# Paired 64-row matmuls on halves of the array become one full 128-row matmul per block of hidden units

## The chip, the cores and the metric

The kernel runs on one core of one Trainium2 chip. The metric is the time of one execution on the device in microseconds (us); the kernel before was run three times.

## The reference

Three stages follow each other: a recurrent attention (mLSTM), a mixture of eight experts with a greedy assignment of tokens, and a dense block.

```python
# attention: 4 batch rows, 8 heads, 768 steps, 40 dims; y = o * (C q) / max(|n q|, 1)
x = y.transpose(0, 2, 1, 3).reshape(3072, 320)
# experts: each takes the 384 tokens that the greedy order of all logits gives it
logits = x @ w_gate
for e in range(8):
    h = np.maximum(x[mask_e] @ w1[e], 0.0)        # 320 -> 1024
    out[mask_e] = h @ w2[e]                       # 1024 -> 320
# dense block on every token
h = out @ w_in                                    # 320 -> 2048
g = np.where(h > 0.0, h, np.exp(np.minimum(h, 0.0)) - 1.0)
return g @ w_out                                  # 2048 -> 320
```

## The kernel before, in words

The attention (class `Attention`) fills the first 224 us. After it come eight rounds (class `Mlp`), one for each expert: a round gathers the 384 tokens of its expert, runs the expert (8 blocks of 128 hidden units) and then the dense block on the same tokens (16 blocks). Class `Router` finds the tokens of the later rounds at the same time; its steps are short products on TensorE (PE, L691, L748, L769, L804 to L806, L831) between chains of small operations on VectorE (DVE).

Every float32 operand is kept as two parts of half the bits, a high one and a low one, and a product of two operands takes three passes: high by high, low by high, high by low. The inner dimension of the first product of both the expert and the dense block is 320, that is two chunks of 128 rows and a last one of 64. `Mlp.up` (L1110) writes one block of 128 hidden units by 384 tokens into a bank of PSUM. For the two chunks of 128 it needs six matmuls (L1118 to L1127). For the last 64 rows the weights `ws` (`w1s` of the expert, `wis` of the dense block) hold both parts above each other: in an even block rows 0 to 63 are the high part and rows 64 to 127 the low one, in an odd block the other way round. The inputs `xh[:, 2]` and `xl[:, 2]` hold the 64 rows twice, above each other. So L1130 does high by high and low by high in one matmul of 128 rows. What is left is high by low, 64 rows. An even block `f` does it for itself on one half of the array (L1136) and for block `f + 1` on the other half (L1137); for that it opens the bank of block `f + 1` ahead of that block's other matmuls:

```python
PE.matmul(p, ws[:64, c], xl[:64, 2], start=False, stop=True)
PE.matmul(self.open_[f + 1][0], ws[64:, c.stop:c.stop + 128], xl[64:, 2], start=new, stop=False)
```

There are (8 + 16) * 8 = 192 blocks, so 96 such pairs. Block by block, `P1` hands the bank to a ReLU (L1157 and L1164) and `P2` to an elu (`elu`: L1189, L1190 on ScalarE, ACT; L1193 on DVE, which is the last reader of the bank; then L996 and L1002, which split the result into `gh` and `gl`). `C1` (L1234 to L1249) and `C2` (L1278 to L1282) take the split blocks three blocks later for the second product. Four banks (`ph`) take turns among the blocks of `up` and the transposes of the next round's tokens (`prep_x`, L1071).

The order of all instructions is settled when the program is built. `Plan` keeps an estimate of each engine's time: `plan.pe(n, cols)` adds n matmuls of `cols` columns to PE's, and the router's steps, the next round's tokens and weights, and the operations that DVE, ACT or GpSimd (POOL) can each do, are put where that estimate says. Each engine then works through its own list in order and waits on semaphores.

Of the kernel before, what the change touches and what calls it, by code (L numbers as in the profile page):

```python
# [18 lines left out]
NR, CAP, TK = 8, 384, 384  # L19
# [16 lines left out]
class Plan:  # L36
    """An estimate of when the engines come to what is emitted (ns), so that nothing is emitted long before its
    operands are there, and what two engines can do goes to the one that is free first."""
# [14 lines left out]
    def on(self, e, ns, after=0):  # L53
        """the time after ns on engine e"""
        self.at[e] = max(self.at[e], self.t, after) + ns
        return self.at[e] + HOP
# [30 lines left out]
class Ring:  # L87
    """The tiles of a tag that take turns: the next one's place is free once its last reader is emitted"""
# [7 lines left out]
    def free(self, k):  # L96
        """whether the next k places are free by now"""
        q = self.q[-self.n:]
        return all(x[0] and x[0] <= self.plan.t for x in q[:max(0, len(q) - self.n + k)])
# [10 lines left out]
def spread(ap, parts):  # L110
    """a run of DRAM for every partition"""
    return bass.AP(tensor=ap.tensor, offset=ap.offset, ap=[[0, parts]] + [list(x) for x in ap.ap])


class Attention:
    """mLSTM by chunks of 128 steps; a unit is a chunk of a batch row with its eight heads"""

    def __init__(self, nc, tc, consts, dram, qko, vk, ig, fg, wg, pad, xd, L, ident):
# [17 lines left out]
        def spin(n):  # L136
            """products of no use that keep the tensor engine's clock up while it waits"""
            for _ in range(n):
                nc.tensor.matmul(junk[:, :4], wz[:, :128], wz, start=True, stop=True)
# [85 lines left out]
    def maximum(self, a, b):  # L225
        """the running maximum that the gates' factors are taken against"""
        if a < b:
            gi, gf, m, _ = self.g
            self.nc.vector.tensor_tensor_scan(m[:, a + 1:b + 1], gf[:, a:b], gi[:, a:b], m[:, a:a + 1], op0=ALU.add,
                                              op1=ALU.max)  # L230

    def parts(self):
        """the later chunks' decay factors as sums of three bfloat16"""
        A, G = self.nc.scalar, self.nc.gpsimd
        gi, gf, m, d1 = self.g
        t = slice(128, S)

        def v3(t):
            return t[:, 128:S].rearrange("p (c t) -> p c t", t=128)

        G.tensor_copy(v3(d1)[:, :, 0:1], v3(gf)[:, :, 0:1])
        G.memset(v3(gf)[:, :, 0:1], 0.0)
        x = gf
        for k in range(3):
            A.activation(self.fp[k * 32:k * 32 + 32, t], x[:, t], AF.Copy)
            if k:
                yield
            if k < 2:
                (self.nc.vector if k else G).tensor_tensor(m[:, t], x[:, t], self.fp[k * 32:k * 32 + 32, t],
                                                           op=ALU.subtract)  # L250
                x = m

    def products(self, c0, c1):
        """the decay factors' running products, from the start of a chunk on"""
        gi, gf, m, d1 = self.g
        t = slice(c0 * 128, c1 * 128)
        self.nc.vector.tensor_tensor_scan(d1[:, t], gf[:, t], d1[:, t], 0.0, op0=ALU.mult, op1=ALU.add)
        for c in range(c0, c1):
            self.nc.sync.dma_start(self.dd[c].rearrange("r h t -> h r t"), d1[:, c * 128:(c + 1) * 128])

    def turn_gi(self, c0, c1):
        """the input factors by token"""
        p = self.pC[:, 256:]
        for c in range(c0, c1):
            self.nc.tensor.transpose(p[:, c * 32:c * 32 + 32], self.g[0][:, c * 128:(c + 1) * 128], self.ident[:32, :32])
# [31 lines left out]
    def scores(self, u, a=0, z=4):  # L297
        """keys by queries, the even heads before the odd ones; a pair of heads on halves of the array"""
        g, b2, c, b = self.U(u)
# [9 lines left out]
    def decay(self, u):  # L309
        """products of the decay factors from each step (partition) to each later one"""  # L310
# [99 lines left out]
    def turn(self, u):  # L410
        """tokens to partitions, and each head's part of the router's logits"""
# [37 lines left out]
    def step(self):  # L449
        """a piece of what others have to do on the vector engine"""  # L450
        while self.extra and next(self.extra[0], self) is self:
            self.extra.pop(0)
# [72 lines left out]
class Router:  # L525
    """The greedy assignment, an expert a round: the one that fills first as the threshold on the tokens'
    best logits falls. The threshold is found digit by digit of the logits' sortable keys. Experts are known by
    weights that fall from 8 to 1, so that the first of several is the heaviest; columns of tokens (a batch row's
    six chunks) run innermost."""
# [57 lines left out]
    def over(x, n):  # L587
        """a factor for every column, over n values"""
        return x.rearrange("p (b g) -> p b g", g=6)[:, :, None].to_broadcast([128, 4, n, 6])

    def values(self, a, n):
        """n values from a on, over the columns"""
# [3 lines left out]
    def cols(t):  # L596
        """[p, n, 24] as [p, 4, n, 6]"""
# [5 lines left out]
    def fold(self, p, z, out, op):  # L603
        """the sum of four blocks of 32 partitions, of z - it if there is a z, and how it compares"""
# [14 lines left out]
    def early(self, c, b0=0, b1=B, digits=None):  # L619
        """the first round's first thresholds, as the logits of batch rows b0..b1 in chunk c come"""  # L620
# [30 lines left out]
    def digits(self, r):  # L651
        """the first two digits of the keys"""
# [27 lines left out]
    def round(self, r):  # L680
        """yields when to go on, whether with the vector engine, and for how long that one idles at least"""
# [164 lines left out]
class Mlp:  # L846
    """Each round's expert on its 384 rows and the dense block behind it. float32 operands are split into two
    parts of half the bits; their products need three passes."""

    def __init__(self, nc, tc, wp, w1a, w1b, w2a, win, wout, xd, out, ident, router, plan):  # L850
# [5 lines left out]
        self.open_, self.half = {}, set()  # L856
# [23 lines left out]
    def conv(self, wide, tiles, sign=False):  # L880
        """float32 of float64 words (float32 stays): the high word's magnitude rescaled by a power of two and
        shifted, the low word's first bits, and the sign as bits or as a factor; yields the vector engine's time"""
        nc = self.nc
        x, g, F = tiles
# [30 lines left out]
    def win_pieces(self, stage):  # L915
        """ten pieces of 512 columns"""
# [46 lines left out]
    def wout_pieces(self):  # L963
        """sixteen blocks of rows"""
# [26 lines left out]
    def copy(self, out, x, a, d):  # L991
        """on the scalar or the vector engine"""
# [6 lines left out]
    def minus(self, out, x, y, d, p, wait=0):  # L999
        """on the vector engine or GpSimd"""  # L1000
# [9 lines left out]
    def get_w(self, r, i):  # L1010
        """a piece of round r's expert's weights"""
# [40 lines left out]
    def psum(self):  # L1052
        """a block of PSUM, once the readers of the one before it in its place are emitted"""
# [3 lines left out]
    def spin(self, n):  # L1057
        """products of no use that keep the tensor engine's clock up while it waits"""
# [3 lines left out]
    def prep_x(self, r):  # L1062
        """round r's rows, turned and split"""
# [46 lines left out]
    def up(self, wh, wl, ws, xh, xl, f):  # L1110
        """a block of 128 hidden units; the products of 64 rows go in pairs of blocks, on halves of the array"""
        PE = self.nc.tensor
        if f in self.open_:
            p, slot = self.open_[f]
        else:
            p, slot = self.open_[f] = self.psum()
        c = slice(f * 128, f * 128 + 128)
        PE.matmul(p, wh[:, 0, c], xh[:, 0], start=f not in self.half, stop=False)  # L1118
        PE.matmul(p, wl[:, 0, c], xh[:, 0], start=False, stop=False)  # L1119
        self.plan.pe(2, TK)  # L1120
        yield 1
        PE.matmul(p, wh[:, 1, c], xh[:, 1], start=False, stop=False)  # L1122
        PE.matmul(p, wl[:, 1, c], xh[:, 1], start=False, stop=False)  # L1123
        self.plan.pe(2, TK)
        yield 2
        PE.matmul(p, wh[:, 0, c], xl[:, 0], start=False, stop=False)  # L1126
        PE.matmul(p, wh[:, 1, c], xl[:, 1], start=False, stop=False)  # L1127
        self.plan.pe(2, TK)
        yield 3
        PE.matmul(p, ws[:, c], xh[:, 2], start=False, stop=f % 2 == 1)  # L1130
        self.plan.pe(1, TK)
        if f % 2 == 0:
            new = f + 1 not in self.open_
            if new:
                self.open_[f + 1] = self.psum()
            PE.matmul(p, ws[:64, c], xl[:64, 2], start=False, stop=True)  # L1136
            PE.matmul(self.open_[f + 1][0], ws[64:, c.stop:c.stop + 128], xl[64:, 2], start=new, stop=False)  # L1137
            self.half.add(f + 1)
            self.plan.pe(2, TK)
        else:  # L1140
            self.half.remove(f)
        del self.open_[f]
        yield p, slot
# [28 lines left out]
    def P2(self, r, fs):  # L1172
        """elu(h) = max(h, exp(min(h, 0)) - 1)"""
# [179 lines left out]
    def prep_xs(self):  # L1353
        """a round's rows once the round before is through with its own"""
# [9 lines left out]
    def prep_ws(self):  # L1364
        """a round's weights once the round before is through with its own"""
# [18 lines left out]
    def start(self, first):  # L1384
        """the first round's assignment, with parts of the dense block's weights in its gaps"""
# [121 lines left out]
def _layout(i):  # L1507
    """The inputs' elements in the order in which the chip reads them."""
# [45 lines left out]
```

## Time and profile before

| | |
|---|---|
| median of the 3 runs | 857.01 us (855.52 to 859.26) |
| the profiled execution: its time on the page, which is the span | 857.0 us |
| PE busy (matmuls) | 761.6 us, 89% of the span |
| DVE busy | 631.2 us, 74% |
| ACT busy | 383.3 us, 45% |
| POOL busy | 281.3 us, 33% |
| mean granted clock of TensorE | 0.942 of full speed |

A row of the timeline gives the start, the duration and the engine, then the line of the kernel, the operation, what it writes and reads, and the shape; in brackets stands how long the engine had been idle before and what ended that. PE is the stream of matmuls and PEld that of their weight loads. Matmuls overlap in the pipeline, so what one costs the stream is the distance from its start to the next one's start and not its duration.

### The profile page before, as it was taken

The numbers are of one execution on the slowest core, as the hardware profiler recorded it, in microseconds if no ns is written. First come the engines' busy times: TensorE is split into PE (matmuls) and PEld (weight loads), VectorE is DVE, ScalarE is ACT, GpSimd is POOL, SyncE is SP. The second block draws the span as 40 slices with busy tenths as digits, with TensorE's granted clock in tenths as the row PEclk, the third lists the DMA queues.
The fourth block names the chain that finished last, engine by engine and source line by source line (L and its number), as shares of the span: only waits on it lengthen the run. The fifth ranks groups of instructions, "written<-read, shape, count | busy, mean of one in ns | idle before, by whom it ended". The sixth has DMA issues, their size and how long they took to land.

```text
span 857.0 us, 14673 instructions
## 1 busy us (share of the span) xinstructions
PE 761.6 (89%) x5417; PEld 671.2 (78%) x5417; DVE 631.2 (74%) x1673; ACT 383.3 (45%) x895; POOL 281.3 (33%) x357
## 2 busy tenths in 40 slices
PE   6878777772789989989999999999999999999995
PEld 4668666761677868878888888888999999899895
DVE  7799999998898985787788769867843752662442
ACT  5445554443436642653364335425623633642431
POOL 6547566314522541350531404311501501111001
PEclk8889889795799989999999999999999999999998
DMA  7678677413521310310310301300310310100000
GB/s 183 194 229 236 193 221 195 121 42 127 167 76 32 117 62 24 98 66 1 125 62 1 125 1 62 102 24 1 120 44 24 111 53 24 62 1 24 1 1 24
DMA packets 21960, 72.30 MB, mean 84 GB/s; under 512 B 3648, under 2 KB 7904, under 8 KB 20912
## 3 DMA queue, kind: packets, MB, share of 16 engines
q1 hardware_dynamic: 13104, 39.15, 16.6%
q0 software_dynamic: 8448, 31.73, 11.2%
q8 instruction: 42, 0.69, 0.3%
q10 hardware_dynamic: 336, 0.49, 0.2%
q14 instruction: 30, 0.25, 0.1%
HBM read 62.62 MB, written 8.73 MB: 83 GB/s over the span
## 4 chain that ended last, share of the span: by engine, by line
PE 53%; DVE 28%; issue 10%; DMA 4%; ACT 2%; POOL 1%; SPq 0%; POOLq 0%; DVEq 0%
PE acc L1278 4%; PE ph L1118 4%; PE acc L1279 4%; PE acc L1282 4%; DVE W L323 3%; PE ph L1136 3%; PE ph L1122 3%; PE ph L1130 3%; PE ph L1126 3%; PE ph L1119 3%; PE ph L1123 3%; PE ph L1127 3%; DVE P L364 2%; PE acc L1247 2%; PE acc L1249 2%
## 5 line engine op out<-in xcount | busy, mean ns | idle before, releaser
L1193 DVE SCALAR_TENSOR_TENSOR e<-e,ph 128x384 f32<-128x384 f32 x128 | 70.1, 551 | 71.0 <-ACT e L1190 69.0
L1278 PE MATMUL acc<-woh,gh 128*128 128x320 f32 x384 | 122.2, 318 | 0.0
L1279 PE MATMUL acc<-wol,gh 128*128 128x320 f32 x384 | 119.0, 310 | 0.0
L1282 PE MATMUL acc<-woh,gl 128*128 128x320 f32 x384 | 118.8, 309 | 0.0
L1189 ACT ACTIVATE e<-ph 128x384 f32<-128x384 f32 x128 | 62.6, 489 | 114.3 <-PE ph L1136 88.3
L1157 ACT ACTIVATE gh<-ph 128x384 fp32r<-128x384 f32 x64 | 31.5, 491 | 131.1 <-PE ph L1136 88.3
L1288 POOL DMA_INDIRECT out_dram<-ot,idx x24 | 23.7, 987 | 188.0 <-ACT ot L994 185.0
L1164 DVE SCALAR_TENSOR_TENSOR gl<-ph,gh 128x384 fp32r<-128x384 f32 x64 | 35.3, 554 | 57.3 <-ACT gh L1157 55.5
L1278 PEld LDWEIGHTS acc<-woh,gh 128*128 128x128 f32 x384 | 72.8, 190 | 1.1 <-issue 0.9
L1279 PEld LDWEIGHTS acc<-wol,gh 128*128 128x128 f32 x384 | 72.6, 189 | 0.0
L1282 PEld LDWEIGHTS acc<-woh,gl 128*128 128x128 f32 x384 | 72.5, 189 | 0.0
L1190 ACT ACTIVATE e<-e 128x384 f32<-128x384 f32 x128 | 67.3, 526 | 4.0
L443 ACT ACTIVATE x<-pT,rd 128x40 f32<-128x40 f32 x184 | 36.4, 309 | 67.8 <-issue 19.4
L417 PE MATMUL pT<-IW,sb 128*128 128x144 f32 x184 | 34.5, 341 | 35.1 <-DVE sb L408 17.8
L1002 DVE TENSOR_TENSOR gl<-e,gh 128x384 fp32r<-128x384 f32 x109 | 63.4, 584 | 1.9
L417 PEld LDWEIGHTS pT<-IW,sb 128*128 128x128 f32 x184 | 28.8, 223 | 38.9 <-ACT x L445 18.5
L323 DVE TENSOR_TENSOR_SCAN W<-pF,id 128x1024 f32<-128x1024 f32 x24 | 54.7, 2278 | 1.5 <-PE pF L315 1.5
L1118 PE MATMUL ph<-yh,wih 128*128 128x384 f32 x128 | 51.8, 405 | 0.4
L1002 POOL TENSOR_TENSOR gl<-e,gh 128x384 fp32r<-128x384 f32 x19 | 20.7, 1091 | 94.4 <-ACT gh L994 36.3
L1122 PE MATMUL ph<-yh,wih 128*128 128x384 f32 x128 | 45.7, 357 | 0.0
L1247 PE MATMUL acc<-gh,w 128*128 128x384 f32 x128 | 44.3, 346 | 0.0
L1126 PE MATMUL ph<-yl,wih 128*128 128x384 f32 x128 | 44.2, 345 | 0.0
(295 smaller groups left out, 2178.4 us busy)
## 6 DMA issues: line engine op xcount, KB each, us to landing
qk<-in_qko_dram SPq DMA_DIRECT2D x22, 480.0 KB
vk<-in_vk_dram SPq DMA_DIRECT2D x12, 640.0 KB
wx<-in_wout_dram SPq DMA_DIRECT2D x16, 320.0 KB
xd<-x SPq DMA_DIRECT2D x22, 192.0 KB
cx<-in_win_dram SPq DMA_DIRECT2D x8, 512.0 KB
db<-dd SPq DMA_DIRECT2D x20, 160.0 KB
cx<-in_win_dram SPq DMA_DIRECT2D x4, 256.0 KB
qk<-in_qko_dram SPq DMA_DIRECT2D x6, 160.0 KB
```

The lines of the kernel that those rows point to most:

```text
L323: self.nc.vector.tensor_tensor_scan(self.W[u].rearrange(fl), p.rearrange(fl), self.id8.rearrange(fl), 0.0, op0=ALU.mult, op1=ALU.add)
L417: self.nc.tensor.matmul(p[:, j, :144], sb[:, j], self.IW[:, j], start=True, stop=True)
L1002: (self.nc.vector if e == "d" else self.nc.gpsimd).tensor_tensor(out, x, y, op=ALU.subtract)
L1118: PE.matmul(p, wh[:, 0, c], xh[:, 0], start=f not in self.half, stop=False)
L1122: PE.matmul(p, wh[:, 1, c], xh[:, 1], start=False, stop=False)
L1126: PE.matmul(p, wh[:, 0, c], xl[:, 0], start=False, stop=False)
L1189: nc.scalar.activation(e, p, AF.Relu, scale=-1.0)
L1190: nc.scalar.activation(e, e, AF.Exp, scale=-1.0)
L1193: nc.vector.scalar_tensor_tensor(e, e, -1.0, p, op0=ALU.add, op1=ALU.max)
L1278: PE.matmul(p, h[:, c], self.woh[:, f], start=f == 0, stop=False)
L1279: PE.matmul(p, h[:, c], self.wol[:, f], start=False, stop=False)
L1282: PE.matmul(p, l[:, c], self.woh[:, f], start=False, stop=f == 15)
```

## The change

Each block does its last 64 rows by itself, as a full matmul of 128 rows: `ws[:, c]` by `xl[:, 2]`, which adds low by low to the high by low that was there. No block opens another's bank, and the bookkeeping for that (`open_`, `half`) goes. The eight matmuls of a block come in four pairs, and `plan.pe(2, TK)` is called four times a block (before, an even block told the plan of nine matmuls and an odd one of seven). The rest of the diff removes docstrings; behind L856 lines move up by one, and behind `up` by 23.

```diff
-        self.open_, self.half = {}, set()
...
     def up(self, wh, wl, ws, xh, xl, f):
         PE = self.nc.tensor
-        if f in self.open_:
-            p, slot = self.open_[f]
-        else:
-            p, slot = self.open_[f] = self.psum()
+        p, slot = self.psum()
         c = slice(f * 128, f * 128 + 128)
-        PE.matmul(p, wh[:, 0, c], xh[:, 0], start=f not in self.half, stop=False)
-        PE.matmul(p, wl[:, 0, c], xh[:, 0], start=False, stop=False)
-        self.plan.pe(2, TK)
-        yield 1
...
-        PE.matmul(p, ws[:, c], xh[:, 2], start=False, stop=f % 2 == 1)
-        self.plan.pe(1, TK)
-        if f % 2 == 0:
-            new = f + 1 not in self.open_
-            if new:
-                self.open_[f + 1] = self.psum()
-            PE.matmul(p, ws[:64, c], xl[:64, 2], start=False, stop=True)
-            PE.matmul(self.open_[f + 1][0], ws[64:, c.stop:c.stop + 128], xl[64:, 2], start=new, stop=False)
-            self.half.add(f + 1)
-            self.plan.pe(2, TK)
-        else:
-            self.half.remove(f)
-        del self.open_[f]
-        yield p, slot
+        for k, (w, x) in enumerate([(wh[:, 0, c], xh[:, 0]), (wl[:, 0, c], xh[:, 0]), (wh[:, 1, c], xh[:, 1]),
+                                    (wl[:, 1, c], xh[:, 1]), (wh[:, 0, c], xl[:, 0]), (wh[:, 1, c], xl[:, 1]),
+                                    (ws[:, c], xh[:, 2]), (ws[:, c], xl[:, 2])]):
+            PE.matmul(p, w, x, start=k == 0, stop=k == 7)
+            if k % 2:
+                self.plan.pe(2, TK)
+                yield (p, slot) if k == 7 else k
```

How the instructions move is shown at three places. The first is PE at the end of an even block of the first round's expert, into the odd block behind it. Before:

```order
L1130 MATMUL ph<-xh,w1s 128x384
L1136 MATMUL ph<-xl,w1s 128x384
L1137 MATMUL ph<-xl,w1s 128x384
L1118 MATMUL ph<-xh,w1h 128x384
L1119 MATMUL ph<-xh,w1l 128x384
L1122 MATMUL ph<-xh,w1h 128x384
L1123 MATMUL ph<-xh,w1l 128x384
L1126 MATMUL ph<-xl,w1h 128x384
L1127 MATMUL ph<-xl,w1h 128x384
L1130 MATMUL ph<-xh,w1s 128x384
```

With the change:

```order
L1117 MATMUL ph<-xh,w1s 128x384
L1117 MATMUL ph<-xl,w1s 128x384
L1117 MATMUL ph<-xh,w1h 128x384
L1117 MATMUL ph<-xh,w1l 128x384
L1117 MATMUL ph<-xh,w1h 128x384
L1117 MATMUL ph<-xh,w1l 128x384
L1117 MATMUL ph<-xl,w1h 128x384 x2
L1117 MATMUL ph<-xh,w1s 128x384
L1117 MATMUL ph<-xl,w1s 128x384
```

The pair of L1136 and L1137 is gone; the even and the odd block now each end with one product of `xl` and `w1s`.

The second place is PE in the dense block of the first round, where the router's ranks are summed (L804 to L806). Before, behind the first two matmuls of an odd block:

```order
L1136 MATMUL ph<-yl,wis 128x384
L1137 MATMUL ph<-yl,wis 128x384
L1118 MATMUL ph<-yh,wih 128x384
L1119 MATMUL ph<-yh,wil 128x384
L804 LDWEIGHTS ones
L804 MATMUL pr<-mm,ones 128x48
L805 LDWEIGHTS tri
L805 MATMUL pr<-mm,tri 128x48
```

With the change (L1255 to L1259 are L1278 to L1282 of before):

```order
L1255 MATMUL acc<-woh,gh 128x320
L1256 MATMUL acc<-wol,gh 128x320
L1259 MATMUL acc<-woh,gl 128x320
L804 LDWEIGHTS ones
L804 MATMUL pr<-mm,ones 128x48
L805 LDWEIGHTS tri
L805 MATMUL pr<-mm,tri 128x48
L806 LDWEIGHTS far
L806 MATMUL pr<-mm,far 128x48
L1117 MATMUL ph<-yh,wih 128x384
```

The router's step stands in front of the even block now and no longer in the odd one behind it, which is eleven matmuls of the main work earlier.

The third place is DVE near the end of the first round's dense block, where a router's chain (L661 to L722) stands in front of L1193, an elu's step that gives a bank free. Before:

```order
L1193 SCALAR_TENSOR_TENSOR e<-e,ph 128x384
L1002 TENSOR_TENSOR w1l<-stg,w1h 128x512
L661 TENSOR_SCALAR u<-b 128x24
L716 TENSOR_TENSOR Lm<-Lm,b 128x4x8x6
L663 TENSOR_TENSOR u<-b,u 128x24
L718 TENSOR_TENSOR Lm<-Lm,kx 128x4x8x6
L671 TENSOR_SCALAR D<-u 128x24 x2
L667 CAST Df<-D 128x48
L721 CAST d<-D 128x24
L722 TENSOR_REDUCE a_704<-Lm 128x24
L1193 SCALAR_TENSOR_TENSOR e<-e,ph 128x384
```

With the change (L1170 is L1193 of before, L1001 and L995 are L1002 and L996):

```order
L995 CAST gh<-e 128x384
L995 CAST xh<-ph 128x3x128
L901 SCALAR_TENSOR_TENSOR wt<-wt 128x320
L661 TENSOR_SCALAR u<-b 128x24
L716 TENSOR_TENSOR Lm<-Lm,b 128x4x8x6
L663 TENSOR_TENSOR u<-b,u 128x24
L718 TENSOR_TENSOR Lm<-Lm,kx 128x4x8x6
L671 TENSOR_SCALAR D<-u 128x24 x2
L667 CAST Df<-D 128x48
L721 CAST d<-D 128x24
L722 TENSOR_REDUCE a_704<-Lm 128x24
L1170 SCALAR_TENSOR_TENSOR e<-e,ph 128x384
```

The chain and the elu's step behind it stay together; in front of the chain stand other operations.

## Rows read from the trace of the kernel before

**Rows 1.** The page's first part: span, and busy time of PE.
```profile
span 857.0 us, 14673 instructions
PE 761.6 (89%) x5417; PEld 671.2 (78%) x5417; DVE 631.2 (74%) x1673; ACT 383.3 (45%) x895; POOL 281.3 (33%) x357
```
**Rows 2.** Busy time by stretch: stretch, length, engines (instructions), granted clock, DMA.
```profile
224.00:300.90 76.90, 69.33 (x420) 58.78 (x419) 70.27 (x195) 41.49 (x87) 31.62 (x32) 0.99 0.24 75
300.90:305.20 4.30, 1.08 (x3) 0.47 (x2) 4.27 (x13) 1.95 (x5) 1.82 (x2) 0.83 0.00 0
305.20:312.00 6.80, 6.80 (x34) 6.47 (x34) 6.13 (x23) 3.62 (x8) 4.15 (x4) 0.61 0.06 10
312.00:618.00 306.00, 296.22 (x1876) 257.51 (x1875) 239.23 (x784) 135.14 (x279) 91.55 (x96) 0.99 0.18 59
618.00:846.00 228.00, 227.81 (x1337) 208.10 (x1336) 109.02 (x221) 92.77 (x189) 30.91 (x39) 1.00 0.11 35
846.00:857.00 11.00, 1.23 (x9) 0.96 (x7) 0.00 (x0) 0.82 (x2) 2.39 (x5) 0.68 0.12 45
```
**Rows 3.** Timeline of PE around a pair in the fourth round.
```profile
512.28 0.33 PE L1130 MATMUL ph<-yh,wis 128*128 128x384 f32 x1
...
512.80 0.34 PE L1130 MATMUL ph<-yh,wis 128*128 128x384 f32 x1
513.07 0.44 PE L1136 MATMUL ph<-yl,wis 64*128 64x384 f32 x1
513.07 0.44 PE L1137 MATMUL ph<-yl,wis 64*128 64x384 f32 x1
513.44 0.44 PE L1118 MATMUL ph<-yh,wih 128*128 128x384 f32 x1
513.72 0.34 PE L1119 MATMUL ph<-yh,wil 128*128 128x384 f32 x1
```
**Rows 4.** Timeline of PEld, the weight loads, around the same pair.
```profile
513.07 0.18 PEld L1136 LDWEIGHTS ph<-yl,wis 64*128 64x128 f32 x1 [0.25 <-issue]
...
513.44 0.19 PEld L1118 LDWEIGHTS ph<-yh,wih 128*128 128x128 f32 x1 [0.18 <-issue]
```
**Rows 5.** Timeline of PE at the end of an odd block, without a pair.
```profile
514.59 0.33 PE L1130 MATMUL ph<-yh,wis 128*128 128x384 f32 x1
514.76 0.30 PE L1278 MATMUL acc<-woh,gh 128*128 128x320 f32 x1
```
**Rows 6.** L1136 by stretch: stretch, length, PE busy (count), PEld busy (count), clock, DMA.
```profile
224.00:300.90 76.90, 4.84 (x11) 2.01 (x11) 0.99 0.24 75
312.00:618.00 306.00, 19.82 (x45) 8.22 (x45) 0.99 0.18 59
618.00:846.00 228.00, 17.16 (x39) 7.12 (x39) 1.00 0.11 35
```
**Rows 7.** Timeline of PE: router's products behind a pair (first, last) and behind L1130.
```profile
327.84 0.17 PE L769 MATMUL pr<-fl,onz 32*128 32x8 bf16 x1
...
573.30 0.47 PE L748 MATMUL pr<-A,ge 128*128 128x32 bf16 x6
...
500.18 0.34 PE L1130 MATMUL ph<-xh,w1s 128*128 128x384 f32 x1
500.45 0.17 PE L769 MATMUL pr<-fl,onz 32*128 32x8 bf16 x1
```
**Rows 8.** Waits of PE from 312 to 618 us: total, times, longest.
```profile
PE pr L748 <- DVE ge L734: 4.4, 4, 3.0
...
PE pr L769 <- DVE fl L617: 1.6, 3, 0.9
```
**Rows 9.** L734, one for each step of the router, by stretch: DVE busy (count).
```profile
312.00:618.00 306.00, 18.96 (x34) 0.99 0.18 59
618.00:846.00 228.00, 0.00 (x0) 1.00 0.11 35
```
**Rows 10.** Timeline of PE: the longest wait of a pair.
```profile
304.62 0.69 PE L1137 MATMUL ph<-yl,wis 64*128 64x384 f32 x1 [3.22 <-DVE e L1193]
```

More of the change, by code (lines that the diff above doesn't have):

```diff
@@ L1112, in up @@
         PE = self.nc.tensor
-        if f in self.open_:
-            p, slot = self.open_[f]
-        else:
-            p, slot = self.open_[f] = self.psum()
+        p, slot = self.psum()
         c = slice(f * 128, f * 128 + 128)
-        PE.matmul(p, wh[:, 0, c], xh[:, 0], start=f not in self.half, stop=False)
-        PE.matmul(p, wl[:, 0, c], xh[:, 0], start=False, stop=False)
-        self.plan.pe(2, TK)
-        yield 1
-        PE.matmul(p, wh[:, 1, c], xh[:, 1], start=False, stop=False)
-        PE.matmul(p, wl[:, 1, c], xh[:, 1], start=False, stop=False)
-        self.plan.pe(2, TK)
[L1125 to L1129, printed above, removed]
-        PE.matmul(p, ws[:, c], xh[:, 2], start=False, stop=f % 2 == 1)
-        self.plan.pe(1, TK)
-        if f % 2 == 0:
-            new = f + 1 not in self.open_
-            if new:
-                self.open_[f + 1] = self.psum()
-            PE.matmul(p, ws[:64, c], xl[:64, 2], start=False, stop=True)
-            PE.matmul(self.open_[f + 1][0], ws[64:, c.stop:c.stop + 128], xl[64:, 2], start=new, stop=False)
-            self.half.add(f + 1)
-            self.plan.pe(2, TK)
-        else:
-            self.half.remove(f)
-        del self.open_[f]
-        yield p, slot
+        for k, (w, x) in enumerate([(wh[:, 0, c], xh[:, 0]), (wl[:, 0, c], xh[:, 0]), (wh[:, 1, c], xh[:, 1]),
[5 more added lines that the diff above has]
+                yield (p, slot) if k == 7 else k
     def parts(self):
```

## The prediction

> **What bounds the kernel now.** I read the page's first part, then cut the rounds into stretches by the busy times, and then went into the timeline of PE. The page says that PE is busy for 761.6 of 857.0 us [rows 1], which is a mean over stages with different limits. By stretches the rounds fall into four [rows 2]. From 224 to 301 us DVE is the fuller engine (70.27 of 76.90 us, with the router's chains, the weights of the dense block and the elus in one list), and PE often waits for it. From 301 to 312 us there is one incident: PE stands still for 4.30 - 1.08 = 3.2 us and then works 6.80 us at a granted clock of 0.61, most of it at 1.2 GHz and not at 2.4. From 312 to 618 us PE is busy for 296.22 of 306.00 us and DVE for 239.23: PE sets the pace, and the 9.8 us of idle time are mostly waits for the router's chains on DVE, at L748 and L769 [rows 8]. From 618 to 846 us the router takes no step any more [rows 9] and PE is busy for 227.81 of 228.00 us: whatever its stream loses or gains there is lost or gained by the kernel. The last 11 us are the scatter of the result and do not change.
>
> **What a pair costs now.** The reader should look at starts. Full matmuls of 384 columns follow each other at (512.80 - 512.28) / 3 = 0.173 us (two rows are left out between) [rows 3]. Around a pair the stream goes differently: from L1130 to the pair 0.27, from the pair to the next matmul 0.37, from that to the one after it 0.28. The two halves do start together at 513.07, so they share the array as written. But the stream pays 0.10 us ahead of them and another 0.10 behind, and the 0.37 of the pair itself is the time of two full matmuls and not of one. The weight loads show why: a load of 128 rows runs under the matmul before it, but that of L1136 begins only with its own matmul, after 0.25 us of idle time, and the 128-row load of L1118 behind the pair again after 0.18, both put down to "issue" and not to any operand [rows 4]. It is not the change of bank that costs this: an odd block ends without a pair, and from its L1130 to the next bank's first matmul it is 0.17 us [rows 5].
>
> **The change part by part.** From L1130 to L1119 a pair takes 513.72 - 512.80 = 0.92 us. With the change the same work is two matmuls more for two blocks at the usual distance: L1130, the even block's last, L1118, and the odd block's last one, four distances of 0.173, that is 0.69. So each pair gives back 0.227 us of PE's stream, although TensorE then does twice the rows for these products.
>
> The Trainium skill speaks against this: its page "TensorE: Matmul & The Clock Gate" says under "Packing small matmuls — row/col tiling" that products of few rows in distinct row groups run at the same time, so that the gain is one of concurrency. By that a pair would cost one matmul, and two full ones would add 0.173 us for each pair where now I take away 0.227. The trace agrees that the halves run together, but not with the price.
>
> By stretches [rows 6]:
> - 618 to 846 us: 39 pairs. PE is never idle there, and what comes behind a matmul (elu, split) has three blocks of time. 39 * 0.227 = **8.9 us**, all on the path.
> - 312 to 618 us: 45 pairs. Ten of them are followed at once by a product of the router (the first at 327.84, the last at 573.30). Such a product has a gap ahead of it anyway (0.27 from L1130 at 500.18 to L769) [rows 7], so I count these ten at nothing: 35 * 0.227 = 7.9 us. What of that reaches the end depends on DVE. The router has 34 steps there [rows 9], with two stops of PE in each (L748 and L769), 68 in all; PE waits in 7 of them [rows 8]. A faster PE comes to each stop some 7.9 / 34 = 0.23 us earlier per step, while DVE, at 78%, has its own chain. The bounds are 0 (DVE paces every stop) and 7.9. I take **6.0**, about three quarters: nine stops in ten did not wait, and some of these will.
> - 224 to 312 us: 11 pairs and the one of the incident. DVE bounds this stretch, so the pairs are worth nothing by themselves (at most 11 * 0.227 = 2.5 us). The incident begins when L1137 wants the next block's bank early and waits 3.22 us for L1193 on DVE [rows 10]. With the change that bank is asked for later, but by the order that I show the chain L661 to L722 still stands ahead of that same step, so some wait of that kind will be there. If it were gone, 3.2 us and the slow clock behind it (6.80 * (1 - 0.61) = 2.7 us) would be won; if it came out twice as long, 3.2 would be lost. I take **0**.
>
> The other edits have one answer. The plan counts 16 matmuls for two blocks before and after, so its clock runs on as it did; it only tells the router's steps and the elus other places, some matmuls earlier in the places shown. DVE, ACT and POOL do the same work, with some splits given to another engine, and none of them is full behind 312 us. Banks are held for a shorter time, which can only help the transposes. An even block now ends a few hundredths earlier and an odd one a matmul later, which the three blocks up to its use cover; without that cover it would be 0.17 us a block.
>
> Sum: 857.0 - 8.9 - 6.0 - 0 = **842 us**. The profiled execution's span is 857.0 us and the median of the runs 857.01, so nothing is to be added.
>
> **The rivals.**
> - *Everything is kept and the incident goes.* 857.0 - 8.9 - 7.9 - 2.5 - 3.2 - 2.7 = 832 us. For it: that wait belongs to the early opening of a bank, which goes. Against: DVE's list there is as full as before.
> - *The router paces the middle.* The 7.9 us go into longer waits at L748 and L769, and only the last stretch gains: 848 us. For it: PE already waits there, and the waits are of the kind that grow when PE is early. Against: the stops that do not wait are many, and a router's step that starts earlier also ends earlier.
> - *The router's stops get worse than that (slower).* The steps are placed earlier in PE's list (eleven matmuls in the place shown), and PE, which works in order, stands still until DVE has its chain. The place is the 68 stops from 312 to 618 us. The whole gain of 16.8 us is gone when each stop waits 0.25 us more than now, and it is 0.5% slower (857.0 + 4.3) from (16.8 + 4.3) / 68 = 0.31 us on. At 0.35 us it would be 857.0 - 16.8 + 23.8 = 864 us. For it: the plan takes no account of what the pairs cost, and PE gets ahead of it less than before. Against: only 7 of 68 stops wait now.
> - *The pair is worth what it looks like (slower).* If the gaps around the pairs are the trace's and not the chip's, or come back around the last full matmul, each pair costs a matmul more: behind 312 us 84 * 0.173 = 14.5 us, 872 us. Against: busy time without gaps fills the last stretch, so the distances add up to the span.
>
> **How the numbers follow.** About 0.5% (4.3 us) is what a measurement of this kernel can tell from no change. Forecast, with 837 to 848 us around it: 0.62. Everything kept: 0.15. The router paces the middle, 848 to 852.7: 0.14. That and a longer wait in the early stretch, so that it ends within 0.5%: 0.04. Slower by the router's stops: 0.03, by the pairs: 0.02. So faster 0.91, same 0.04, slower 0.05. The range goes from 833 (both later stretches in full, 840, and nearly all of the early 8.4) to 851 (only the last stretch kept, 848, and an early wait longer by 3).
>
> **What would show it.** In the last stretch: matmuls of `up` at 0.173 us throughout, no weight load behind "issue" at the block's end, and some 9 us less from the end of the router to the end. In the middle: PE idle for 10 to 14 us in place of 9.8, at L748 and L769. In the early stretch: a PE wait for L1193's counterpart of about 3 us and a granted clock of 1.2 GHz behind it. I am wrong if the last full matmul of a block starts more than 0.2 us behind the one before it, or if waits for DVE grow by more than 8 us.

## The result, and the profile after

| | median | runs |
|---|---|---|
| before | 857.59 us | 855.52 to 859.26 (4) |
| with the change | 844.12 us | 839.18 to 845.87 (4) |

The ratio is 0.9835, with a 95% interval from 0.9801 to 0.9868: 13.5 us less. The profiled execution of the change has a span of 843.0 us, and its own time is 844.81 us. The first part of its page:

```profile
span 843.0 us, 14709 instructions
PE 744.5 (88%) x5417; PEld 694.1 (82%) x5417; DVE 626.7 (74%) x1669; ACT 378.8 (45%) x884; POOL 296.8 (35%) x373
```

TensorE still issues 5417 matmuls and is busy for 17.1 us less than before [rows 1]. Some small operations went from DVE and ACT to POOL; the run in the old order below, where they did not, took as long.

The pair is gone from the stream. The timeline of PE at the end of an even block (L1117 at 507.14 is the block's last matmul) and into the next one, and of PEld at another block's end:

```profile
506.97 0.34 PE L1117 MATMUL ph<-yh,wis 128*128 128x384 f32 x1
507.14 0.38 PE L1117 MATMUL ph<-yl,wis 128*128 128x384 f32 x1
507.36 0.34 PE L1117 MATMUL ph<-yh,wih 128*128 128x384 f32 x1
507.54 0.35 PE L1117 MATMUL ph<-yh,wil 128*128 128x384 f32 x1
```

```profile
412.56 0.19 PEld L1117 LDWEIGHTS ph<-xh,w1s 128*128 128x128 f32 x1
412.73 0.19 PEld L1117 LDWEIGHTS ph<-xl,w1s 128*128 128x128 f32 x1
412.91 0.14 PEld L1211 LDWEIGHTS acc<-gl,w 128*64 128x64 f32 x1
413.09 0.19 PEld L1213 LDWEIGHTS acc<-gh,w 128*128 128x128 f32 x1
```

Three distances take 507.54 - 506.97 = 0.57 us where L1130, the pair and L1118 took 0.92 [rows 3]; at most places it is nearer to 3 * 0.175. No load of `up` waits behind "issue" any more, as those of L1136 and L1118 did [rows 4]; the router's short products still have such loads. The third load shown has 64 columns in place of 128 but all 128 rows, and the loads around it keep their distance of 0.17 to 0.18: fewer columns bring no gap here.

To compare stretches with the same work, both traces are cut where `C1` of a round starts (L1232 before, L1209 after). Busy time by stretch, before and then after: the first round, rounds two to five, the rest up to the last products.

```profile
224.55:324.36 99.81, 88.71 (x529) 75.66 (x529) 90.74 (x259) 51.38 (x108) 41.39 (x43) 0.96 0.22 70
324.36:644.22 319.86, 310.38 (x1956) 271.49 (x1956) 239.06 (x775) 139.29 (x286) 91.11 (x95) 0.99 0.18 57
644.22:846.00 201.78, 201.59 (x1180) 184.09 (x1180) 99.04 (x200) 83.87 (x171) 27.55 (x33) 1.00 0.10 32
```

```profile
225.77:323.19 97.42, 86.41 (x535) 79.83 (x535) 86.79 (x255) 51.23 (x109) 47.31 (x49) 0.94 0.22 70
323.19:637.43 314.24, 302.64 (x1954) 282.09 (x1952) 237.75 (x774) 135.83 (x278) 97.99 (x103) 0.99 0.18 58
637.43:832.00 194.57, 194.40 (x1180) 191.07 (x1180) 101.10 (x200) 82.88 (x168) 29.65 (x36) 1.00 0.10 33
```

The last stretch is 7.2 us shorter, with PE idle for 0.2 us in it before and after. In the middle PE is busy for 7.7 us less, but its idle time grows from 9.5 to 11.6 us, so 5.6 us are left. The first round is 2.4 us shorter and begins 1.2 us later; PE is busy for 2.3 us less in it and idle for as long as before (11.0 us, and 11.1 before). The sum is 14.0 us, the difference of the two spans.

The idle time of the middle stretch is where it was, at the router's stops. Waits of PE there (in all, times, longest), before and then with the change:

```profile
PE pr L748 <- DVE ge L734: 4.1, 3, 3.0
PE pr L691 <- DVE X L688: 2.5, 3, 1.3
PE pr L769 <- DVE fl L617: 1.6, 3, 0.9
PE pr L831 <- DVE R L824: 0.9, 1, 0.9
```

```profile
PE pr L748 <- DVE ge L734: 5.2, 3, 3.5
PE pr L831 <- DVE R L824: 2.1, 2, 1.2
PE pr L691 <- DVE X L688: 2.0, 2, 1.2
PE pr L769 <- DVE fl L617: 2.0, 3, 0.8
```

The incident of the first round is still there too, at another instruction. The timeline of PE with the change, and two stretches of busy time behind it:

```profile
303.60 0.90 PE L1070 MATMUL ph<-ident,xg 128*128 128x128 f32 x3 [4.59 <-DVE e L1170]
304.16 0.99 PE L1117 MATMUL ph<-yl,wih 128*128 128x384 f32 x2
304.94 0.52 PE L1117 MATMUL ph<-yh,wis 128*128 128x384 f32 x1
305.26 0.52 PE L1117 MATMUL ph<-yl,wis 128*128 128x384 f32 x1
```

```profile
304.00:308.00 4.00, 4.00 (x16) 3.74 (x14) 3.97 (x17) 2.65 (x7) 2.54 (x3) 0.50 0.33 97
308.00:312.00 4.00, 4.00 (x30) 3.65 (x29) 2.95 (x11) 2.96 (x7) 1.32 (x2) 0.91 0.61 230
```

The transposes of the next tokens now wait 4.59 us for the elu's step on DVE that gives a bank free, in place of 3.22 at L1137 [rows 10]. After it the granted clock is 0.50, the level of 1.2 GHz, and the distance of matmuls is 0.32 us until it is back.

### The profile page after: what moved, and what is told of

Read it like the earlier page. It is cut to its first block, busy times and chain, and to the rows that moved or that the text cites. A ratio compares the mean times of both kernels' runs of the same rounds, so it can differ in the third digit from the quotient of the medians.

```text
span 843.0 us, 14709 instructions
## 1 busy us (share of the span) xinstructions
PE 744.5 (88%) x5417; PEld 694.1 (82%) x5417; DVE 626.7 (74%) x1669; ACT 378.8 (45%) x884; POOL 296.8 (35%) x373
## 4 chain that ended last, share of the span: by engine, by line
PE 55%; DVE 31%; issue 7%; ACT 3%; DMA 3%; POOL 0%; SPq 0%; POOLq 0%; DVEq 0%; ACTq 0%
PE ph L1117 23%; PE acc L1255 5%; DVE W L323 4%; PE acc L1259 4%; PE acc L1256 4%; PE acc L1224 3%; PE acc L1226 2%; PE acc L1225 2%; DVE P L364 2%; DVE e L1170 2%; DMA qk<-in_pad_dram 2%; PE pr L748 2%; DVE gl L1001 1%; PE acc L1211 1%; DVE ge L734 1%
## 5 line engine op out<-in xcount | busy, mean ns | idle before, releaser
L1255 PE MATMUL acc<-woh,gh 128*128 128x320 f32 x384 | 123.2, 321 | 0.0
L1259 PE MATMUL acc<-woh,gl 128*128 128x320 f32 x384 | 120.2, 313 | 0.0
L1170 DVE SCALAR_TENSOR_TENSOR e<-e,ph 128x384 f32<-128x384 f32 x128 | 69.9, 549 | 62.2 <-ACT e L1167 61.2
L1001 POOL TENSOR_TENSOR gl<-e,gh 128x384 fp32r<-128x384 f32 x33 | 34.7, 1055 | 165.5 <-DVE gh L995 130.1
L1117 PE MATMUL ph<-yh,wih 128*128 128x384 f32 x256 | 90.3, 353 | 0.4
L1117 PE MATMUL ph<-yh,wil 128*128 128x384 f32 x256 | 86.8, 339 | 0.0
L1259 PEld LDWEIGHTS acc<-woh,gl 128*128 128x128 f32 x384 | 72.9, 190 | 0.6
L1255 PEld LDWEIGHTS acc<-woh,gh 128*128 128x128 f32 x384 | 73.1, 190 | 0.2
L1117 PE MATMUL ph<-yl,wih 128*128 128x384 f32 x256 | 66.9, 342 | 0.0
L1001 DVE TENSOR_TENSOR gl<-e,gh 128x384 fp32r<-128x384 f32 x95 | 57.3, 607 | 1.9
L1117 PEld LDWEIGHTS ph<-yh,wih 128*128 128x128 f32 x256 | 48.8, 191 | 4.4 <-ACT yh L1229 4.4
```

What stands on the lines that cost most here:

```text
L1001: (self.nc.vector if e == "d" else self.nc.gpsimd).tensor_tensor(out, x, y, op=ALU.subtract)
L1117: PE.matmul(p, w, x, start=k == 0, stop=k == 7)
L1170: nc.vector.scalar_tensor_tensor(e, e, -1.0, p, op0=ALU.add, op1=ALU.max)
L1255: PE.matmul(p, h[:, c], self.woh[:, f], start=f == 0, stop=False)
L1259: PE.matmul(p, l[:, c], self.woh[:, f], start=False, stop=f == 15)
```

## The experiments

The theory: the cost sits at the change from matmuls of 128 rows to matmuls of 64 and back. The main rival: the gain comes from the other order and from banks that are opened later. The change itself was timed again in one batch with three of the runs (full rows in the old order, a lone half, full rows in the router's products). The other two were timed in a second batch, where the kernel before took 859.23 us.

> The change as it is, timed beside the other kernels of this batch. About 844 us, ratio 0.983 to 0.986 to the kernel before.

Measured: 844.16 us, ratio 0.9844 (0.9812 to 0.9875). The expected came, and this is the base for the comparisons below.

**Full rows in the old order.** The kernel before, with two operands widened:

```diff
-            PE.matmul(p, ws[:64, c], xl[:64, 2], start=False, stop=True)
-            PE.matmul(self.open_[f + 1][0], ws[64:, c.stop:c.stop + 128], xl[64:, 2], start=new, stop=False)
+            PE.matmul(p, ws[:, c], xl[:, 2], start=False, stop=True)
+            PE.matmul(self.open_[f + 1][0], ws[:, c.stop:c.stop + 128], xl[:, 2], start=new, stop=False)
```

> The kernel before with nothing changed but the rows of the pair: both matmuls take 128 rows, at their old places and into the banks opened as early as before; every engine's list stays as it was, row for row. Theory (the gaps belong to the change from 128-row to 64-row matmuls and back): 0.92 us from L1130 to L1119 become 0.69, the late rounds go from 69.95 us to about 67.4, and the whole comes to 840 to 846 us, like the change. Rival (the gain comes from the new order and from banks opened later): 855 to 859 us. If both have a part, between the two.

Measured: 844.69 us, ratio 0.9835 (0.9803 to 0.9868), the same as the change. Every engine's list is that of the kernel before, the banks are opened as early, and the late rounds take 67.40 us where they took 69.95 (from one `C1` to the next). Busy time of the middle and the last stretch there:

```profile
324.42:637.67 313.25, 302.09 (x1956) 281.33 (x1956) 238.86 (x775) 139.18 (x286) 91.54 (x95) 0.99 0.18 59
637.67:832.20 194.53, 194.35 (x1180) 191.08 (x1180) 99.08 (x200) 83.98 (x170) 27.96 (x33) 1.00 0.10 33
```

So the rows of the matmuls carry the whole gain, and order and banks have no part in it that these runs could tell. What the order does is only to move waits about: here PE waits 3.4 us at L1137 for L1193, much as in the kernel before, and 2.2 us at L1232 for a split on DVE, which the change does not have. The first round gains 1.1 us where the change gains 2.4, and the middle stretch 6.6 where the change gains 5.6.

**A lone half.** The change, with the last product on 64 rows:

```diff
+        h = slice(f % 2 * 64, f % 2 * 64 + 64)
...
-                                    (ws[:, c], xh[:, 2]), (ws[:, c], xl[:, 2])]):
+                                    (ws[:, c], xh[:, 2]), (ws[h, c], xl[h, 2])]):
```

> The change, but the last product of each block takes only its 64 rows of high by low, on the lower or the upper half of the array, one after the other and without a partner (low by low is left out as in the kernel before). Theory: every block now pays the gap ahead and the gap behind. If a lone half costs what the pair cost (0.37 us), a block takes 0.92 where it took 3 * 0.173 = 0.52, 0.40 more, 192 * 0.40 = 77 us, 905 to 922 us. If the lone half itself takes 0.17, 0.20 more a block, 38 us, 875 to 885 us. Rival (rows are free, what counts is the number of matmuls): 842 to 847 us, as the change.

Measured: 898.65 us, ratio 1.0476 (1.0422 to 1.0529), 54 us more than the change. The timeline of PE in a late round:

```profile
700.52 0.34 PE L1118 MATMUL ph<-yh,wis 128*128 128x384 f32 x1
700.79 0.44 PE L1118 MATMUL ph<-yl,wis 64*128 64x384 f32 x1
701.16 0.44 PE L1118 MATMUL ph<-yh,wih 128*128 128x384 f32 x1
701.44 0.34 PE L1118 MATMUL ph<-yh,wil 128*128 128x384 f32 x1
```

The distances are 0.27, 0.37 and 0.28, to the hundredth those of the pair: a lone half costs what a pair costs, so the second half of a pair is free, and the 0.40 us over three usual distances is there without a partner. That it is the price of going to 64 rows and back, and not of every 64-row matmul, the next run tells. The rival that rows cost nothing falls. The total is 6 us below the range that I gave, because I put all 192 blocks on the path. In the late stretch it fits: the 68 blocks there cost 220.92 - 194.53 = 26.4 us, 0.39 each (194.53 us in the change timed beside it). In the middle the 96 blocks cost 339.00 - 314.24 = 24.8 us, only 0.26 each, in the main because the slower stream swallowed waits for the router: PE is idle for 2.9 us there, against 11.6 in the change.

```profile
325.88:664.88 339.00, 336.07 (x1953) 278.32 (x1951) 236.99 (x774) 137.03 (x278) 97.38 (x103) 0.99 0.17 54
664.88:885.80 220.92, 220.75 (x1180) 188.45 (x1180) 99.47 (x200) 83.61 (x168) 30.34 (x36) 1.00 0.09 29
```

**A second pair behind the first.** The kernel before, with the two lines of the pair in a loop:

```diff
-            PE.matmul(p, ws[:64, c], xl[:64, 2], start=False, stop=True)
-            PE.matmul(self.open_[f + 1][0], ws[64:, c.stop:c.stop + 128], xl[64:, 2], start=new, stop=False)
+            for k in range(2):
+                PE.matmul(p, ws[:64, c], xl[:64, 2], start=False, stop=k == 1)
+                PE.matmul(self.open_[f + 1][0], ws[64:, c.stop:c.stop + 128], xl[64:, 2], start=new and k == 0, stop=False)
```

> The kernel before, with each pair of 64-row matmuls issued twice in a row (the product of the last 64 rows, high by low, is added twice). Theory (the cost sits at the change from 128 rows to 64 and back): the second pair starts a usual distance of 0.17 to 0.18 us behind the first and its weight load runs under the first, 96 * 0.175 = 17 us, 868 to 875 us. Rival (every 64-row matmul pays, its weight load never runs under the one before): 0.37 us between the two pairs, 96 * 0.37 = 36 us, 886 to 894 us. Rival (a pair costs two matmuls because its halves in truth run one after the other): 0.35 us, 885 to 893 us.

Measured: 871.14 us, ratio 1.0145 (1.0114 to 1.0177). The timelines of PE and PEld (L1136 and L1137 of before are L1137 and L1138 there):

```profile
660.10 0.34 PE L1130 MATMUL ph<-xh,w1s 128*128 128x384 f32 x1
660.37 0.44 PE L1137 MATMUL ph<-xl,w1s 64*128 64x384 f32 x1
660.38 0.44 PE L1138 MATMUL ph<-xl,w1s 64*128 64x384 f32 x1
660.65 0.33 PE L1137 MATMUL ph<-xl,w1s 64*128 64x384 f32 x1
660.66 0.33 PE L1138 MATMUL ph<-xl,w1s 64*128 64x384 f32 x1
660.92 0.44 PE L1118 MATMUL ph<-xh,w1h 128*128 128x384 f32 x1
661.20 0.34 PE L1119 MATMUL ph<-xh,w1l 128*128 128x384 f32 x1
```

```profile
660.37 0.18 PEld L1137 LDWEIGHTS ph<-xl,w1s 64*128 64x128 f32 x1 [0.26 <-issue]
...
660.48 0.19 PEld L1137 LDWEIGHTS ph<-xl,w1s 64*128 64x128 f32 x1
...
660.91 0.19 PEld L1118 LDWEIGHTS ph<-xh,w1h 128*128 128x128 f32 x1 [0.25 <-issue]
```

From L1130 to L1119 it is 1.10 us with two pairs and 0.92 with one: the second pair adds 0.18, a usual distance, and its load starts at 660.48 under the first pair. It does not start a usual distance behind the first pair, as I expected, but 0.28 behind it, and the matmul behind it comes 0.27 later where it was 0.37. So the four distances are 0.27 and 0.28 around the change to 64 rows, and 0.27 and 0.28 around the change back: 0.10 too much ahead of each and 0.10 behind, 0.20 us for a change of rows. The 64-row loads do run ahead, as long as the matmul before them has 64 rows too; only the first load behind a change of rows waits. Both rivals (every 64-row matmul pays; the halves run one after the other) fall: each would have made the 1.10 us at least 1.27. The whole is some 12 us over the kernel before and not 17: a late round takes 2.2 us more for its 12 second pairs, the 0.18 of the rows, and less came through in the earlier stretches. If a third pair added as much as the second, a run of k pairs would cost 0.40 + 0.17 k us and replace 2 k full matmuls at 0.17 each, so that, as an estimate from one and two pairs, they would begin to win from the third in a row on. With four banks for the blocks no more than two can stand in a row here, so this was not tried.

**Full rows in the router's products.** The same cost should sit at L769, whose products have 32 rows. The change, with 96 rows of zeros added in two tiles that keep them:

```diff
+        self.flz = [c.tile([128, 8], BF, name=f"flz{i}") for i in range(2)]
+        for t in self.flz:
+            G.memset(t, 0.0)
...
-                fl = self.T([128, 8], BF, "fl")
+                fl = self.flz[i % 2] if i or r else self.T([128, 8], BF, "fl")
...
-                    K = 32
-                    self.fold(pk[:, :32].rearrange("p (i b) -> p b i", b=4), rem, fl[:K], ALU.is_ge)
+                    K = 128
+                    self.fold(pk[:, :32].rearrange("p (i b) -> p b i", b=4), rem, fl[:32], ALU.is_ge)
```

> The change, and the router's products of 32 rows at L769 get 128 rows, of which 96 are zeros kept in two tiles of their own. Theory: the gap of 0.10 us ahead of L769 goes (0.27 to 0.17 from the matmul before it, where PE does not wait), 40 of them lie in the rounds, so up to 4 us; as many stops wait for VectorE, 0 to 3 us less than the change in the same batch, 841 to 844 us. Rival (the gap ahead of L769 comes from its short bfloat16 product, not from its rows): the gap stays at 0.27 and the time is that of the change.

Measured: 838.55 us, ratio 0.9779 (0.9747 to 0.9811), 5.6 us less than the change beside it (844.16) and more than the 0 to 3 that I expected. The same stop of the router in the timeline of PE, with the change and then with full rows (L1120 and L772 there are L1117 and L769):

```profile
442.39 0.33 PE L1117 MATMUL ph<-yh,wil 128*128 128x384 f32 x1
442.66 0.17 PE L769 MATMUL pr<-fl,onz 32*128 32x8 bf16 x1
442.76 0.44 PE L1117 MATMUL ph<-yh,wih 128*128 128x384 f32 x1
443.04 0.34 PE L1117 MATMUL ph<-yh,wil 128*128 128x384 f32 x1
```

```profile
438.74 0.34 PE L1120 MATMUL ph<-yh,wil 128*128 128x384 f32 x1
438.92 0.18 PE L772 MATMUL pr<-flz,onz 128*128 128x8 bf16 x1
438.96 0.42 PE L1120 MATMUL ph<-yh,wih 128*128 128x384 f32 x1
439.22 0.33 PE L1120 MATMUL ph<-yh,wil 128*128 128x384 f32 x1
```

The stop takes 0.48 us in place of 0.65: 0.09 is won ahead of the product and 0.08 behind it, and I had counted the first alone. The product is bfloat16 as before, so the rival falls. In the middle stretch, with 32 of the 42 such products, PE is busy for 5.5 us less than in the change beside it (302.57 us there), as 32 * 0.17 = 5.4 has it, and the waits, which I expected to grow, stay: 12.1 us idle, 11.6 there. The long distance behind the next full matmul (0.26) stays too; no run tells why. This is the fastest version of the study.

**The plan at the measured distance.** The run before, with a dearer matmul in the plan, so that only the plan's choices move:

```diff
-        self.t += n * (cols / 2.4 + 3)
+        self.t += n * (cols / 2.4 + 14)
```

> The run with full rows in the router's products, and the plan's price of a matmul raised from columns / 2.4 + 3 ns to columns / 2.4 + 14 ns, that is 0.174 us for 384 columns, as measured; nothing else, so only the order of the instructions moves. Theory (PE's waits for the router grow because the plan lets PE come too early): TensorE's idle time in the middle rounds falls from 12 us to 7 to 10, 833 to 837 us. Rival (the waits are set by how full VectorE is, whatever the order): 837 to 841 us; a worse order could also give more.

Measured: 850.71 us, ratio 0.9901 (0.9873 to 0.9928): slower than the run that it is built on. Busy time of the middle stretch in the run that it is built on, and then here:

```profile
321.53:630.70 309.17, 297.05 (x1954) 279.46 (x1952) 237.64 (x774) 135.69 (x278) 98.12 (x103) 0.99 0.18 59
327.23:643.49 316.26, 298.49 (x1943) 279.46 (x1943) 240.43 (x773) 132.16 (x270) 94.01 (x98) 0.99 0.17 58
```

PE's idle time is 316.26 - 298.49 = 17.8 us, where it was 12.1. The stretch is 7.1 us longer, and the first round takes 4.3 us more. The theory that the waits come from the plan's low price falls; that they depend on how full DVE is and not on the order falls as well, as the plan alone, which sets the order and which engine takes some small operations, moved them by some 6 us. Which step of it does so stays open.

## Why the prediction was right

I forecast 842 us in a range from 833 to 851, and the runs gave 844.12. By its own steps:

- *The price of a pair* (0.92 against 0.69, 0.227 us back): the last stretch holds 34 pairs in the cut used here and gave back 7.2 us, 0.212 each. Full matmuls do not keep to 0.173 everywhere (0.22 once in the rows above).
- *The last stretch, 8.9 us for 39 pairs*: at 0.212 it is 8.3. Right in kind, 7% too large. The sign that I named for being wrong, a block's last matmul more than 0.2 us behind the one before it, did not come: it is 0.17 in the rows above.
- *The middle, 6.0 of 7.9 us*: the stream became 7.7 us shorter, and 5.6 came through. This cut holds 48 pairs, and 7.7 us is 0.212 for 36 of them; so counting the ten with a router's product behind them at nothing was about right. The rest went into longer waits for the router, 11.6 us in place of 9.5, inside the 10 to 14 that I named; with the old order 6.6 came through. A third of these waits is at L691 and L831, stops that I had not counted. In the run with the plan at the measured distance the plan's choices alone cost more than the quarter that I had set aside, so the three quarters were no more than a fair guess.
- *The first round, 0*: it gave 2.4 us, and the attention ahead of it ended 1.2 later. The later start is no effect of the change: two profiles of the change itself start at 223.54 and 225.77 us. My reason for the zero was that DVE bounds this stretch, so that a shorter stream of PE would only wait longer. That did not come: PE is busy for 2.3 us less over the 14 pairs of this cut, and its idle time stayed at 11 us. The waits only changed places: the one of 2.1 us at L1232 went, those at L748 grew by 1.9. Which engine sets this stretch stays open: with a lone half in each block PE is busy for 7.6 us more in it than in the change beside it, and it is only 1.6 us longer. The incident stayed, as expected, at 4.59 us for some 3.
- *The sum*: I set the span equal to the time. For the change the profiled execution took 844.81 us against a span of 843.0, so the span is some 2 us short of the time; the difference of the two kernels is not touched by this. I forecast a gain of 14.9 us, the medians gave 13.5 and the two profiles 14.0. That the total fits so well is in part luck: the two later stretches were taken somewhat too high and the first too low, and the start of the first round, which has nothing to do with the change, took 1.2 us back.

The rival by which a pair is worth what it looks like fell at the price, not at the mechanism: the halves do share the array, and a lone one costs as much as both. The Trainium skill has both sides. Its page "TensorE: Matmul & The Clock Gate", under "Packing small matmuls — row/col tiling", counts on the concurrency, which these traces confirm: the halves start together, and the pair takes no longer than a lone half. The Trainium skill's page "TensorEngine Tiling (Array Packing)", under "Key Properties", says that changing the tiling mode drains the engine; it names no price. The runs show 0.20 us for each change of rows here, 0.40 for a pair among full matmuls; whether the engine empties in that time they do not show. The rival of the router's stops fell too: their waits grew by 2 us and not by 17.

## What to carry to other kernels

Packing two half-height matmuls beside each other did not pay here, and by the estimate above it would only with three or more such pairs in a row; one pair among full matmuls costs more than two full ones, because the stream pays at both changes of rows. So look in the timeline at the distances from start to start on both sides of a matmul with fewer rows, and then at weight loads that wait for "issue". The load alone is no sign: with full rows in the router's products it still waits 0.16 us for "issue", and the product starts at the usual 0.18. Filling the rows up, with zeros or with a product that does no harm, can be cheaper. What a shorter stream gives in a stretch with waits for another engine is less than its sum, and the idle time before and after tells how much less.

## What the runs showed of the hardware

A lone 64-row matmul of 384 columns among full ones cost 0.40 us more than a full one would in the same place, and a pair exactly as much. A load for 64 columns and 128 rows, in contrast, kept the stream at its usual distance. Inside a run of 64-row matmuls the loads ran ahead again (0.18 us for a second pair). Going to 64 rows and going back cost 0.20 us each, half of it ahead of the first matmul with the other number of rows and half behind it. A product of 32 rows paid on both sides as well, 0.17 us for a stop, though it has only 8 columns. And after PE had stood still for 4.59 us, the granted clock was 0.50 over the next 4.00 us and 0.91 in the 4.00 after them.
